# Filler matmuls, a transposed u in PSUM, earlier weights and another load order in the first batch of a recurrent-attention-plus-MLP kernel

## The chip, the cores and the metric

The kernel runs on one core of one Trainium2 chip. The metric is device time in microseconds (us). Medians are over all runs of a kernel, ratios over its fast runs alone. Most executions of one kernel agree within about 1%. A run that is over 1.5% above the fastest of the same kernel is marked slow and left out of the ratios. Engine names in the profile: PE is TensorE (matmul), PEld its weight load, DVE is VectorE, ACT ScalarE, POOL GpSimd, SP SyncE. An engine name with a q is its sequencer issuing a DMA. L325 is line 325 of that kernel's file, so the same operation has another line number in each kernel.

## The reference, cut to what matters

```
# q, k, v, alpha: [4, 8, 768, 48] float32
for t in range(S):                                   # gated linear recurrence, per batch and head
    state = alpha[:, :, t, :, None] * state + k[:, :, t] (outer) v[:, :, t]
    y[:, :, t] = q[:, :, t] @ state
x = y as [batch, 768, 384]
h = x^T @ U @ V                                      # low-rank token mix, rank 32
u = x + h^T
out = u + relu(u @ w_ch1) @ w_ch2                    # MLP 384 -> 1536 -> 384
```

The kernel handles the recurrence in chunks of 128 steps, six per batch and 24 in all. A chunk needs one tile each of alpha, k, q and v. A tile is 128 partitions of eight head rows of 192 bytes, 192 KB together.

## The kernel before

All operations are first put in a list with estimated durations. A small planner then simulates the engines at build time, and writes each engine's instructions in the order that it found. On the chip this order is fixed: an instruction whose data is late holds up everything behind it on its engine, even if that could run. For the planner, DMA is a pipe that serves in order: each input tile takes 1030 ns of it.

```python
    # the planner's DMA model, in Plan.run
            if eng == "SP":                          # input tiles and outputs, on the sync queue
                dma = max(dma, t + 600.0) + cost
                clock[eng] = max(t + 450.0, dma - 3500.0)
                end = dma + 1600.0
            elif op.mode == "DMA":                   # weights, issued by GpSimd
                clock[eng] = t + 1000.0
                dma = max(dma, t + 1000.0) + cost
                end = max(t + 1000.0 + cost, t) + 2000.0
    # ... cut ...
    io = Pool(slots("io", 36, [C, H, D], FP32))      # landing tiles of the inputs
    # ... cut ...
    nc.scalar.dma_start(u_in, moe_U.rearrange("(c p) r -> p c r", p=128))
    for g in range(4):                               # V four times, for four row groups
        nc.scalar.dma_start(v_in[32 * g : 32 * g + R, :], moe_V)
    # ... cut: one chunk, stage_gla(b, c) ...
        # lt = log(alpha), ScalarE; its cumulative sum over time by a triangular matmul on TensorE
        P.add({"ACT": 435}, lambda e: nc.scalar.activation(lt()[:, :, 0:D], at(), AF.Ln), ...)
            nc.tensor.matmul(cb()[:, 0:DM], lhsT=ut_ones, rhs=lt()[:, :, 0:D], ...)
        # ai = exp(-sum), aa = exp(sum); rk = k * ai, rq = q * aa; both transposed; scores; y
    # ... cut: the token mix, stage_mix(b) ...
        # H = V^T (U^T x); ub = x + H; ub transposed by TensorE into PSUM, copied to uT; then the MLP
    # ... cut: the weights, with the last chunk of batch 0 ...
                vt = tiles[b, c][3]                  # three parts of w_ch1 follow v(0,5)
                for i in range(3):
                    P.add({"POOL": 2000}, lambda e, i=i: f_w1(i), r=[vt], w=[("w1", i)], ..., mode="DMA")
                vt = tiles[1, 0][3]                  # three parts of w_ch2 follow v(1,0)
                for i in range(3):
                    P.add({"POOL": 2400}, lambda e, i=i: f_w2(i), r=[vt], w=[("w2", i)], ..., mode="DMA")
```

k(0,5) below means the k tile of batch 0, chunk 5.

## Time and profile before

| | before |
|---|---|
| median of 3 runs | 186.41 us (185.22 to 186.91) |
| profiled span | 186.9 us |
| first MLP matmul starts | 43.99 us |
| last y matmuls of batch 0 start | 36.56 us |

The page of the kernel before has these lines besides those that the prediction shows. The first is the input queue: packets, megabytes, and the time its packets took as a share of 16 DMA engines over the span. The second is the chain of work that ended last, by engine. The last two are issues: size of one, and median us from issue to landing.

```profile
q1 hardware_dynamic: 103296, 23.60, 60.5%
...
PE 72%; DVE 5%; DMA 3%; issue 1%; ACT 1%; DVEq 0%; ACTq 0%
...
io<-in_alpha_dram SPq DMA_DIRECT2D x24, 192.0 KB, 3.8
...
w_sb<-in_moe_w_ch_dram POOLq DMA_DIRECT2D x6, 384.0 KB, 10.2
```

The chain is TensorE work for 72% of the span, so the end was set by TensorE. The first line gives a figure that matters later: 60.5% of 16 times 186.9 us, over 103296 packets, is 17.5 ns per packet.

### The profile page before, as it was taken

Reading aid. Unit: us, or ns where it says so; the run is one execution under the profiler, and the core shown is the slowest. Engines: PE = TensorE matmul, PEld = TensorE weight load, DVE = VectorE, ACT = ScalarE, POOL = GpSimd, SP = SyncE. Lnnn points to the kernel's source line nnn. Section 1 sums busy time; section 2 is a strip of 40 time slices with the busy share of each in tenths; the row PEclk is TensorE's granted clock in tenths of the full one; section 3 lists DMA queues with packets and bytes.
Section 4 is the critical chain, followed back from the end, with each engine's and each line's share of the span. In section 5 each row is a group of like instructions: output and inputs, shape, how many; then the busy total and the mean of one; then the engine's idle time right before and its main releaser. Section 6 shows DMA issues by size and latency. Waiting matters only on the chain.

```text
span 186.9 us, 4147 instructions
## 1 busy us (share of the span) xinstructions
PE 163.1 (87%) x1592; PEld 105.7 (57%) x1592; DVE 93.5 (50%) x185; ACT 98.8 (53%) x229; POOL 57.4 (31%) x86
## 2 busy tenths in 40 slices
PE   0157878788999999889999969999999999999991
PEld 0135655455666666566666647667666466665660
DVE  1137665546810667489687395546665462100321
ACT  2423555436897445669788829215876200797000
POOL 4061445774130444444464309510700000000000
PEclk9999999999999999999999996999999999999999
DMA  6999999999996689899899989952000112200222
GB/s 135 212 201 216 200 192 196 182 198 186 187 192 137 137 208 214 186 219 204 163 195 183 193 174 221 209 173 84 4 0 0 46 42 84 84 4 0 84 84 86
DMA packets 107075, 26.71 MB, mean 143 GB/s; under 512 B 101168, under 2 KB 106928, under 8 KB 107056
## 3 DMA queue, kind: packets, MB, share of 16 engines
q1 hardware_dynamic: 103296, 23.60, 60.5%
q0 software_dynamic: 2784, 2.36, 8.0%
q10 hardware_dynamic: 976, 0.49, 1.2%
q8 instruction: 12, 0.20, 0.4%
q14 instruction: 7, 0.06, 0.1%
HBM read 24.08 MB, written 4.72 MB: 154 GB/s over the span
## 4 chain that ended last, share of the span: by engine, by line
PE 72%; DVE 5%; DMA 3%; issue 1%; ACT 1%; DVEq 0%; ACTq 0%
PE ps L472 25%; PE ps L496 25%; PE ps L337 5%; PE ps L358 3%; DMA io<-in_alpha_dram 3%; PE ps L409 3%; DVE pm L368 2%; PE ps L450 2%; DVE ub L441 2%; PE ps L308 2%; PE ps L440 2%; PE ps L383 1%; PE ps L407 1%; PE ps L381 1%; PE ps L311 1%
## 5 line engine op out<-in xcount | busy, mean ns | idle before, releaser
L472 PE MATMUL ps<-uT,w_sb 128*128 128x384 bf16 x288 | 51.9, 326 | 0.0
L496 PE MATMUL ps<-w_sb,h1t 128*128 128x384 bf16 x288 | 51.6, 326 | 0.0
L483 ACT ACTIVATE h1t<-ps 128x384 bf16<-128x384 f32 x78 | 37.8, 490 | 19.3 <-PE ps L472 19.2
L326 POOL TENSOR_TENSOR rk<-io,ai 128x384 bf16<-128x384 f32 x24 | 21.9, 912 | 49.7 <-ACT ai L319 44.4
L496 PEld LDWEIGHTS <-h1t 128*128 128x128 bf16 x288 | 26.6, 98 | 16.1 <-issue 0.3
L368 DVE TENSOR_TENSOR pm<-ps,maskc 128x512 bf16<-128x512 f32 x48 | 31.2, 685 | 8.1 <-PE ps L358 8.0
L472 PEld LDWEIGHTS <-w_sb 128*128 128x128 bf16 x288 | 26.3, 98 | 15.6
L503 DVE TENSOR_TENSOR ou<-ub,ps 128x384 f32<-128x384 bf16 x24 | 13.3, 554 | 34.4 <-PE ps L496 34.0
L301 ACT ACTIVATE lt<-io 128x384 bf16<-128x384 f32 x24 | 12.7, 529 | 12.7 <-DMA io<-in_alpha_dram 8.3
L319 ACT ACTIVATE ai<-ps 128x384 bf16<-128x384 f32 x24 | 11.9, 498 | 13.9 <-PE ps L311 6.8
L261 POOL CAST rv<-io 128x384 bf16<-128x384 f32 x24 | 13.1, 547 | 17.6 <-DMA io<-in_v_dram 17.6
L326 POOL TENSOR_TENSOR rq<-io,aa 128x384 bf16<-128x384 f32 x18 | 16.5, 915 | 2.1 <-PE ps L472 2.1
L308 PE MATMUL ps<-lt,ut_ones 128*128 128x384 bf16 x24 | 9.3, 391 | 8.6 <-ACT lt L301 8.5
L257 ACT CAST xb<-ps 128x384 bf16<-128x384 f32 x23 | 11.1, 482 | 9.7 <-PE ps L409 9.7
L393 DVE TENSOR_TENSOR st<-ps,tot 128x384 bf16<-128x384 f32 x20 | 11.1, 554 | 8.4 <-PE ps L383 8.4
L337 PE MATMUL ps<-ident,rk 128*128 128x128 bf16 x96 | 11.1, 249 | 2.8 <-POOL rk L326 2.8
L441 DVE TENSOR_TENSOR ub<-xb,ps 128x384 bf16<-128x384 bf16 x24 | 11.6, 547 | 2.6 <-PE ps L440 2.6
L409 PE MATMUL ps<-rv,pm 128*128 128x48 bf16 x192 | 10.6, 192 | 2.5 <-DVE pm L368 2.5
L358 PE MATMUL ps<-qt,kt 48*128 48x128 bf16 x192 | 10.8, 240 | 2.2 <-DVE qt L259 2.1
L485 DVE TENSOR_SCALAR h1t<-ps 128x384 bf16<-128x384 f32 x18 | 9.6, 556 | 6.1 <-PE ps L472 5.8
L257 ACT COPY kt<-ps 128x512 bf16<-128x512 bf16 x14 | 8.2, 588 | 7.8 <-PE ps L337 7.7
L337 PE MATMUL ps<-ident,rq 128*128 128x128 bf16 x96 | 10.8, 244 | 1.7 <-DVE rq L326 1.6
(52 smaller groups left out, 166.0 us busy)
## 6 DMA issues: line engine op xcount, KB each, us to landing
io<-in_alpha_dram SPq DMA_DIRECT2D x24, 192.0 KB, 3.8
io<-in_k_dram SPq DMA_DIRECT2D x24, 192.0 KB, 3.9
io<-in_q_dram SPq DMA_DIRECT2D x24, 192.0 KB, 3.9
io<-in_v_dram SPq DMA_DIRECT2D x24, 192.0 KB, 3.9
out_dram<-ou SPq DMA_DIRECT2D x24, 192.0 KB, 1.9
w_sb<-in_moe_w_ch_dram POOLq DMA_DIRECT2D x6, 384.0 KB, 10.2
v_in<-in_moe_V_dram ACTq DMA_DIRECT2D x4, 96.0 KB, 4.3
u_in<-in_moe_U_dram ACTq DMA_DIRECT2D x1, 96.0 KB, 3.6
```

What stands on the lines that cost most here:

```text
L257: nc.scalar.copy(dst, src)
L261: nc.gpsimd.tensor_copy(dst, src)
L326: eng.tensor_tensor(dst()[:, :, 0:D], a(), x(), op=ALU.mult)
L337: nc.tensor.matmul(t[:, p, :], lhsT=ring()[:, 2 * p : 2 * p + 2, :].rearrange("t h w -> t (h w)"), rhs=ident, start=True, stop=True, is_tr ...
L358: nc.tensor.matmul(sc[par]()[:, p * C : (p + 1) * C], lhsT=kT()[o : o + D, p, :], rhs=qT()[o : o + D, p, :], start=(p == 0), stop=(p == HP ...
L368: nc.vector.tensor_tensor(pm()[:, :, par, :], s2, maskc.to_broadcast([C, HP, C]), op=ALU.mult)
L409: nc.tensor.matmul(y[:, h * D : (h + 1) * D], lhsT=pm()[:, h // 2, h % 2, :], rhs=rv()[:, h, :], start=(h == 0 and sprev is None), stop=(h ...
L441: P.add({"DVE": 465}, lambda e, c=c, hb=hb: nc.vector.tensor_tensor(ub()[:, c, :], xb()[:, c, :], hb()[:, 0:DM], op=ALU.add), r=[hb, (xb, ...
L472: nc.tensor.matmul(hb()[:, 0:TW], lhsT=w1_sb[jt * 128 // FW][:, ct, jt * 128 % FW : jt * 128 % FW + 128], rhs=uT()[:, ct, tt * TW : (tt + ...
L483: nc.scalar.activation(dst, hb()[:, 0:TW], AF.Relu)
L496: nc.tensor.matmul(hb()[:, 0:DM], lhsT=h1()[:, jt, c * C : (c + 1) * C], rhs=w2_sb[jt // JW][:, jt % JW, :], start=(jt == 0), stop=(jt == ...
L503: P.add({"DVE": 468}, lambda e: nc.vector.tensor_tensor(ou(), ub()[:, c, :], hb()[:, 0:DM], op=ALU.add), r=[hb, (ub, c)], w=[ou], prio=-100)
```

## The change

Its intent: bring the MLP of batch 0 forward. TensorE runs cold and with gaps in the first batch, so fillers should keep its clock up. V is loaded once and spread to four row groups by a small matmul. The transposed u of batch 0 is built directly in PSUM. The weights are issued once k(0,5) has landed, earlier than before, and v of a chunk is loaded behind alpha, k and q of the next one, except in the last chunk of a batch. The planner's weight and tile costs are changed to match. The diff, cut:

```diff
@@ planner: weights have a pipe of their own beside the tiles'
             elif op.mode == "DMA":
-                clock[eng] = t + 1000.0
-                dma = max(dma, t + 1000.0) + cost
-                end = max(t + 1000.0 + cost, t) + 2000.0
+                clock[eng] = t + 900.0
+                big = max(big, t + 1500.0) + cost
+                dma = max(dma, t + 1500.0) + cost
+                end = big + 1600.0
@@ fillers in 60% of the planned TensorE gaps, up to 33 us of planned time
+        at = self.warm_from
         for op in order:
+            if op.eng == "PE" and op.t < self.warm_until:
+                n = int((op.t - at - 100.0) * self.warm_share / 216.0)
+                for _ in range(n):
+                    self.warm()
+            if op.eng == "PE":
+                at = op.t + op.engs["PE"]
             op.fn(op.eng)
@@ tiles
-    v_in = const.tile([128, S], FP32, name="v_in")
+    v_in = const.tile([R, S], FP32, name="v_in")
+    v_bf = const.tile([R, S], BF16, name="v_bf")
 ...
+    filler = const.tile([128, 512], BF16, name="filler")
+    nc.vector.memset(filler, 0.0)
+    tiny = const.tile([128, 1], FP32, name="tiny")
@@ loads
-            P.add({"SP": 1030.0}, lambda e: nc.sync.dma_start(t(), ...), w=[t], prio=key)
+            P.add({"SP": 965.0}, lambda e: nc.sync.dma_start(t(), ...), w=[t], prio=key)
 ...
-            for t, src, o in ((at, alpha, 0.0), (kt, k, 0.1), (qt, q, 0.2), (vt, v, 1.05)):
+            for t, src, o in ((at, alpha, 0.0), (kt, k, 0.1), (qt, q, 0.2), (vt, v, 1.25 if c < NC - 1 else 0.3)):
@@ scales and the cast of v on either of two engines in batch 0
-        P.add({"POOL": 885}, ... rk ...)
-        P.add({"DVE": 420} if b == 0 else {"POOL": 885}, ... rq ...)
+        both = {"DVE": 420, "POOL": 885} if b == 0 else {"POOL": 885}
+        P.add(both, ... rk ...)
+        P.add(both, ... rq ...)
@@ mix of batch 0: x transposed into PSUM, H^T accumulated on it, copied to uT (ub follows later)
+                def f_x(e, j, ...): nc.tensor.matmul(tb[j]()[...], lhsT=xb()[:, c, j * C : (j + 1) * C], rhs=ident, ...)
+                def f_h(e, j, ...): nc.tensor.matmul(tb[j]()[:, 0:TW], lhsT=utx()[:, j * C : (j + 1) * C], rhs=vm_sb[...], ...)
@@ weights
-                vt = tiles[b, c][3]
-                ... three parts of w_ch1 after v(0,5), three of w_ch2 after v(1,0)
+                kt = tiles[b, c][1]
+                P.add({"POOL": 100}, lambda e: nc.gpsimd.tensor_copy(tiny, kt()[:, 0, 0:1]), r=[kt], w=["gate"], prio=-1)
+                for i in range(2):
+                    P.add({"POOL": 2200 * (i + 1)}, lambda e, i=i: f_w1(i), r=["gate"], w=[("w1", i)], prio=-1, mode="DMA")
+                P.add({"POOL": 7000}, lambda e: f_w2(), r=["gate"], w=["w2"], prio=-1, mode="DMA")
```

## The prediction

> **What bounds the kernel now.** I read the busy tenths in 40 slices of the page first, to see whether one limit holds all along. It does not:
>
> ```profile
> PE   0157878788999999889999969999999999999991
> POOL 4061445774130444444464309510700000000000
> DMA  6999999999996689899899989952000112200222
> ```
>
> A slice is 4.67 us. From slice 9 (42 us) on the TensorE is full, and the DMA is full until 127 us. Before 42 us the TensorE shows 70 to 80% busy, which looks harmless; the by-line view of the two transposes of a chunk, taken for 12 to 40 us and again for 45 to 105 us, says what those tenths are made of (durations min/median/max in ns):
>
> ```profile
> L337 PE MATMUL ps<-ident,rk x22: 281/314/314, 11.8 to 33.0; 128*128 128x128 bf16 x22
> L308 PE MATMUL ps<-lt,ut_ones x6: 478/500/527, 12.0 to 35.1; 128*128 128x384 bf16 x6
> L337 PE MATMUL ps<-ident,rk x44: 218/219/230, 46.8 to 100.2; 128*128 128x128 bf16 x44
> L308 PE MATMUL ps<-lt,ut_ones x11: 322/326/326, 47.0 to 100.5; 128*128 128x384 bf16 x11
> ```
>
> The same instruction takes 314 ns early and 219 ns late, and 500 against 326: the array runs cold through the whole first batch. The difference for 384 columns, about 174 ns, is 384 columns at half rate against full rate. The timeline of the TensorE then shows the period of the recurrence and where warmth begins:
>
> ```profile
> 17.35 0.50 PE L308 MATMUL ps<-lt,ut_ones 128*128 128x384 bf16 x1
> 21.14 0.61 PE L358 MATMUL ps<-qt,kt 48*128 48x128 bf16 x8 [0.52 <-DVE qt L259]
> 21.68 0.50 PE L308 MATMUL ps<-lt,ut_ones 128*128 128x384 bf16 x1
> 26.01 0.50 PE L308 MATMUL ps<-lt,ut_ones 128*128 128x384 bf16 x1
> 38.64 2.08 PE L440 MATMUL ps<-utx,vm_sb 128*128 128x384 bf16 x6 [0.57 <-ACT utx L257]
> 43.99 1.14 PE L472 MATMUL ps<-uT,w_sb 128*128 128x384 bf16 x6
> ```
>
> A chunk takes 4.33 us (17.35 to 21.68 to 26.01). The bulk work, the first MLP matmul (L472), starts only at 43.99. The issues on the sync queue say whether data is late: alpha is issued every 3.95 us between 8.12 and 31.81, and the last input of batch 0 is issued at 25.16, some 3.9 us (the page's median landing) before it lands at about 29. Its y is finished only at 37.06 (copy xb). So the first batch is bound by a **chain of latencies in static order** (cumulative sum, exp, scale, transpose, copy out, scores, next sum), not by DMA alone. It also starts late; two waits show why (total us, times, longest):
>
> ```profile
> ACT lt L301 <- DMA io<-in_k_dram: 4.3, 1, 4.3
> POOL vm_sb L269 <- DMA v_in<-in_moe_V_dram: 5.0, 1, 5.0
> ```
>
> ScalarE spends 1.28 to 6.25 issuing four copies of V before its first log at 6.30, and GpSimd waits for the fourth copy (to 9.81) before it can scale the first k (10.60).
>
> After 44 us the end is set by TensorE throughput: the MLP matmuls are a half of the ending chain, 0.163 us each. Count it, with columns/2.4 GHz plus 2.5 ns each (the rate at which 72 matmuls took 11.70 us at the chain's end): a chunk 1.77 us, a mix 2.4 us, an MLP 144 x 0.1625 = 23.4 us per batch (72 + 72 matmuls). From 44 to 183 us lie four MLPs (93.6), some 17.5 chunks (31) and three mixes (7.2): 132 us of 139, so 7 us are lost. Two places hold most of it: 76 to 86 us, where MLP of batch 0 has run out and batch 1's mix is not ready, and 110.7 to 112.3, where the TensorE waits for an alpha tile.
>
> **What the Trainium skill says.** "TensorE: Matmul & The Clock Gate", Part 1: the array's default clock is half, released after some 3.4 us of sustained activity, lost after an idle window; back to back, a matmul takes N/1.2 ns cold and N/2.4 + 2.5 ns warm. The trace agrees: 174 ns difference for 384 columns against 157.5 by the formula, and six H matmuls at 38.64 span 2.08 us where later six take 1.14; the granted clock in the page reads 9 throughout and does not show this. "DMA: Bandwidth & Descriptors", Issuing engines are not separate DMA queues: all queues share the 16 engines and interleave. The trace agrees: once the weights are issued (32.5 to 38.7 us), the next input issues take 5.23, 5.42 and 4.14 us instead of about 0.9. "SBUF — State Buffer", Who interferes with whom: a VectorE instruction with two SBUF inputs contends with a GpSimd one that reads SBUF. The scale rq on VectorE takes 0.55 us alone and 0.73 to 0.81 beside a GpSimd scale here, so moving rk to VectorE too is not free of that.
>
> **The change part by part.**
>
> *Fillers.* Matmuls of 512 columns on zeros into a reserved eighth bank, 60% of the planned gaps up to 33 us of planned time. Planned free time is about 33 - 1.5 - 6 x 1.77 = 21 us; 60% of it by 0.216 is at most 58, fewer after rounding down, say 40. If they warm the array, each cycle loses 0.15 us in the sum, 0.1 to 0.2 in each of two transposes, 0.2 in the scores: about 0.6 of 4.33, so 3.7 us. Inputs at 3.85 us per chunk (four tiles of 0.965) then bind equally. The cost is delay where a real gap is shorter than planned, some tenths, mostly in the first 5 us while each cold filler takes 0.43 us.
>
> *V once, on the sync queue.* Removes 3 x 96 KB (1.5 tiles, some 1.4 us of DMA), frees ScalarE from 1.3 to 6.2 and GpSimd from its wait to 9.8. First log near 4.2 instead of 6.3; scores of chunk 0 near 8 to 9 instead of 12.7. Two selection matmuls and two copies rebuild V on four row groups (0.16 + 0.48 us each), off the path.
>
> *Load order and rk on either engine.* v(5) moves ahead of the next batch's alpha. Fitting the trace (28.5 tile equivalents landed by 28.6 us: 1.24 + 0.96 n), k(5) now lands near 22.4, q(5) 23.3, v(5) 25.2. Scale on VectorE 0.56 against 0.91.
>
> *First MLP.* Chain-limited, chunk 5's scores come 5 x 3.75 = 19 us after those of chunk 0, so at 27 to 28; data-limited at 25.5. Then masks 1.3, y 0.35, xb 0.5, utx 0.5, its copy 0.5, with hand-over about 0.1 each: H near 31.
>
> *u transposed in PSUM.* Before: H 38.64, ub adds, transposes, copies, MLP at 43.99, 5.35 us. After: x transposed by identity ahead of time (18 matmuls), H accumulated on it (six times 0.16), three copies of 0.5 us per half on two engines: about 1.5 us. The six ub matmuls and adds (1.0 us of TensorE) stay but move behind.
>
> So the first MLP matmul moves from 44.0 to **32.5** (30.5 to 35): 11.5 us gained.
>
> *Weights.* Issued after k(5), near 22.5 to 24. All take about 14 us of DMA (the tiles slow from 32.5 to 52 while some five come through). First part (512 columns) lands near 29, second near 34, needed 2 us after the start, third by 42, needed 12 us after. Just in time. Input tiles for batch 1 now starve from 24 to 42 rather than 33 to 52.
>
> **The sum.** Of 11.5 us, 1.0 goes back for ub and 0.8 for the sums and transposes of batch 1 that used to precede 44 us. That leaves 9.7. Batch 1 ends landing at 41.5 + 20.5 x 0.98 = 61.6, plus 9 us of chain, so its mix ends at 70 to 72, where before it ended at 85.5; the TensorE needs 32.5 + 23.4 + 1 + 10.6 = 67.5 plus bubbles. So 2 to 4 us of waiting remain at that hand-over, slightly fewer than before. From there to the end 97 to 99 + 3.9 us tail: 173 to 176; alternatively 186.4 - 9.7 = 176.7. I choose **175.5 us** (-5.9%).
>
> **The rivals.** *DMA becomes the bound.* Alpha of batch 3's fourth chunk landed at 111.7; with 1.5 us less V and no sync-queue stall (56.8 to 61.6, where an output in queue order blocks input issues) it lands near 106, 5 us earlier, while the TensorE arrives 10 us earlier. Static order then puts the difference into waits: 0 to 4 us, giving up to 180. For it: tiles took 1.05 us each from 85 to 106 us while the new plan assumes 0.965. Against it: TensorE still has batch 2's MLP to run, if it is ordered first. *Fillers don't warm, or delay.* The array was up to 80% busy and still cold. Then the period stays near 4.2, MLP starts at 36 and runs cold for its first microseconds: 179 to 180. *Weights late.* If batch 1's tiles keep the weights from coming, MLP stalls at its second part by 2 to 4 us: 178 to 180. *More gain.* If the hand-over to batch 1 loses nothing and alpha is in time, the 7 us lost shrink to 4: 171.
>
> **Range and chances.** Most rivals cost less than the 9.7 us; all together would be needed to lose them. Range 170.5 to 181. Two per cent is 182.7: faster 0.91, same 0.07, slower 0.02.
>
> **What would show it.** Transposes of 219 ns before 30 us (warm); first log at 4 to 5; L472's first matmul at 32.5 with copies of uT straight after H; the weight tile waited for not at all; mix of batch 1 done near 71; a TensorE wait for alpha near 106. I am wrong if the early transposes stay at 314, if the MLP starts after 36, or if waits for input tiles past 60 us add to more than 8 us.

## The result

| | before | after |
|---|---|---|
| median | 186.34 us (4 runs) | 198.67 us (4 runs, 197.25 to 199.83) |
| profiled span | 186.9 us | 197.4 us |
| last y matmuls of batch 0 start | 36.56 us | 33.01 us |
| first MLP matmul starts | 43.99 us | 51.43 us |
| from there to the end of the span | 142.9 us | 146.0 us |

The changed kernel is **slower**, by a ratio of 1.067 (95% interval 1.056 to 1.077). Here and below, a ratio is the mean time of one kernel's fast runs over that of the other's in the same rounds, so not quite the ratio of the medians quoted. The predicted time was 175.5 us, with a range up to 181.

Of the 10.5 us between the two profiled spans, 7.4 lie before the first MLP matmul and 3.1 after it. Yet batch 0's recurrence ended 3.5 us earlier. So something came in between.

### The profile after

The page of the changed kernel, lines that answer to those of before (tenths in 40 slices of 4.93 us; PEclk is the granted clock in tenths):

```profile
PE   6976978006999999989988997599999999999991
...
PEclk9999589655999999999999999969999999999999
DMA  6999999999993199999999989942200012200222
...
q1 hardware_dynamic: 104128, 23.80, 65.7%
...
PE 35%; SPq 23%; issue 17%; DMA 11%; POOL 10%; ACT 1%; DVE 1%; POOLq 0%; ACTq 0%
...
io<-in_alpha_dram SPq DMA_DIRECT2D x24, 192.0 KB, 4.5
...
w_sb<-in_moe_w_ch_dram POOLq DMA_DIRECT2D x1, 1152.0 KB, 17.5
```

The two zeros in the PE line are a hole of some 11 us, from 35 to 46 us, while DMA is full. PEclk falls to 5 or 6 in the hole and right behind it, and once before, around 20 to 25 us. It is no sure sign of a cold array: in the kernel before it reads 9 all through the first batch, where transposes take 314 ns. The DMA line has a hole of its own at slices 12 and 13 (59 to 69 us). The chain that ended last is no longer mostly TensorE: the sync queue's issues (SPq) take 23%. And the input queue's packets take 65.7% of 16 times 197.4 us over 104128, which is 19.9 ns each, where before had 17.5.

The timeline of TensorE around the hole (start, length, the group, in brackets the idle time before it and what ended that):

```profile
33.01 0.35 PE L434 MATMUL ps<-rv,pm 128*128 128x48 bf16 x7 [0.40 <-DVE pm L393]
...
34.44 0.39 PE L362 MATMUL ps<-ident,rk 128*128 128x128 bf16 x4
46.14 0.48 PE L332 MATMUL ps<-lt,ut_ones 128*128 128x384 bf16 x1 [11.31 <-ACT lt L325]
...
46.59 1.44 PE L473 MATMUL ps<-vm_sb,utx 128*128 128x384 bf16 x4
...
51.43 1.79 PE L521 MATMUL ps<-uT,w_sb 128*128 128x384 bf16 x10
```

L473 is H accumulated on the transposed x of **batch 0**, and everything it needs is there at about 35 (the copy utx ends at 34.92). In front of it stands L332, the cumulative sum of chunk (1,1), of the **next batch**. It waits 11.31 us for a log, and the timeline of ScalarE says why the log is late:

```profile
45.56 0.52 ACT L325 ACTIVATE lt<-io 128x384 bf16<-128x384 f32 x1 [12.47 <-DMA io<-in_alpha_dram]
```

GpSimd's timeline shows what filled the DMA in this time, and the sync queue's shows the alpha tile's issue:

```profile
27.40 0.19 POOL L564 COPY tiny<-io 128x1 f32<-128x1 f32 x1 [2.56 <-DMA io<-in_q_dram]
27.53 1.71 POOL L299 DMA_DIRECT2D w_sb<-in_moe_w_ch_dram  x2
29.24 1.05 POOL L302 DMA_DIRECT2D w_sb<-in_moe_w_ch_dram  x1
```

```profile
28.89 1.00 SPq L310 DMA_DIRECT2D io<-in_alpha_dram  x1
29.93 2.68 SPq L310 DMA_DIRECT2D io<-in_k_dram  x1
32.66 9.14 SPq L310 DMA_DIRECT2D io<-in_q_dram  x1
...
57.91 0.75 SPq L310 DMA_DIRECT2D io<-in_v_dram  x1
67.18 0.37 SPq L552 DMA_DIRECT2D out_dram<-ou  x1
```

Alpha(1,1) was issued at 28.89, between the weights, and used at 45.56: some 16.7 us from issue to landing, where the median is 4.5. The later lines show the follow-up. Between 58.7 and 67.2 the sync queue issues nothing. Next in its order stands the first output of batch 0, which is late because the MLP is; 8.5 us, where the same stall before took 4.7. This is the hole in the DMA line.

The sums of waits (total us, times, longest), first of the kernel before, then of the changed one:

```profile
ACT lt L301 <- DMA io<-in_alpha_dram: 8.3, 6, 3.6
```

```profile
ACT lt L325 <- DMA io<-in_alpha_dram: 23.9, 12, 12.5
...
PE ps L332 <- ACT lt L325: 12.9, 4, 11.3
```

What the change was made for did work. The by-line view of the transposes of rk, and of the fillers, from 5 us (durations min/median/max in ns):

```profile
L362 PE MATMUL ps<-ident,rk x24: 219/253/314, 6.0 to 29.6; 128*128 128x128 bf16 x24
```

```profile
L273 PE MATMUL ps<-filler x29: 376/390/634, 1.2 to 33.2; 128*128 128x512 bf16 x29
```

The fillers warm the array, though not all along: 219 ns is the warm transpose, 314 the cold one, and those that start between 19.66 and 25.8 us are slow again.

### The profile page after: what moved, and what is told of

It is laid out like the page before. It is cut to its first block, busy times and chain, and to the rows that moved or that the text cites. A ratio compares the mean times of both kernels' runs of the same rounds, so it can differ in the third digit from the quotient of the medians.

```text
span 197.4 us, 4236 instructions
## 1 busy us (share of the span) xinstructions
PE 168.4 (85%) x1629; PEld 104.3 (53%) x1629; DVE 94.9 (48%) x188; ACT 102.7 (52%) x237; POOL 53.5 (27%) x83
## 3 DMA queue, kind: packets, MB, share of 16 engines
q1 hardware_dynamic: 104128, 23.80, 65.7%
## 4 chain that ended last, share of the span: by engine, by line
PE 35%; SPq 23%; issue 17%; DMA 11%; POOL 10%; ACT 1%; DVE 1%; POOLq 0%; ACTq 0%
SPq L310 22%; PE ps L544 18%; PE ps L521 12%; DMA io<-in_alpha_dram 9%; POOL rq L350 4%; POOL rk L350 4%; POOL rv L284 2%; DMA io<-in_k_dram 2%; PE ps L482 1%; PE ps L362 1%; PE ps L383 1%; PE ps L492 1%; SPq L287 1%; ACT lt L325 0%; PE ps L332 0%
## 5 line engine op out<-in xcount | busy, mean ns | idle before, releaser
L531 ACT ACTIVATE h1t<-ps 128x384 bf16<-128x384 f32 x84 | 40.4, 492 | 24.9 <-PE ps L521 24.8
L521 PE MATMUL ps<-uT,w_sb 128*128 128x384 bf16 x288 | 50.8, 326 | 0.4 <-ACT uT L280 0.4
L350 POOL TENSOR_TENSOR rk<-io,ai 128x384 bf16<-128x384 f32 x22 | 20.1, 913 | 59.4 <-ACT ai L343 59.4
L350 POOL TENSOR_TENSOR rq<-io,aa 128x384 bf16<-128x384 f32 x21 | 19.2, 914 | 10.4 <-DMA io<-in_q_dram 6.7
L332 PE MATMUL ps<-lt,ut_ones 128*128 128x384 bf16 x24 | 8.4, 353 | 13.0 <-ACT lt L325 12.9
L284 POOL CAST rv<-io 128x384 bf16<-128x384 f32 x18 | 9.1, 506 | 17.3 <-DMA io<-in_v_dram 14.9
L282 DVE COPY qt<-ps 128x512 bf16<-128x512 bf16 x16 | 6.8, 423 | 13.2 <-PE ps L362 13.2
L273 PE MATMUL ps<-filler 128*128 128x512 bf16 x29 | 11.0, 495 | 1.2 <-DVE offd L241 1.2
L362 PE MATMUL ps<-ident,rq 128*128 128x128 bf16 x96 | 10.2, 234 | 2.0 <-DVE rq L350 1.5
L344 ACT ACTIVATE aa<-ps 128x384 bf16<-128x384 f32 x24 | 11.9, 495 | 0.0
L362 PE MATMUL ps<-ident,rk 128*128 128x128 bf16 x96 | 10.0, 231 | 1.3 <-DVE rk L350 0.8
L434 PE MATMUL ps<-rv,pm 128*128 128x48 bf16 x192 | 9.2, 185 | 1.7 <-DVE pm L393 0.9
## 6 DMA issues: line engine op xcount, KB each, us to landing
w_sb<-in_moe_w_ch_dram POOLq DMA_DIRECT2D x1, 1152.0 KB, 17.5
```

The costliest lines, as they stand in the source:

```text
L284: nc.gpsimd.tensor_copy(dst, src)
L344: P.add({"ACT": 390}, lambda e: nc.scalar.activation(aa().rearrange("t h d -> t (h d)"), cb()[:, 0:DM], AF.Exp), r=[cb], w=[aa], prio=pr + ...
L350: eng.tensor_tensor(dst()[:, :, 0:D], a(), x(), op=ALU.mult)
L362: nc.tensor.matmul(t[:, p, :], lhsT=ring()[:, 2 * p : 2 * p + 2, :].rearrange("t h w -> t (h w)"), rhs=ident, start=True, stop=True, is_tr ...
L521: nc.tensor.matmul(hb()[:, 0:TW], lhsT=w1_sb[i][:, ct, o : o + 128], rhs=uT()[:, ct, tt * TW : (tt + 1) * TW], start=(ct == 0), stop=(ct = ...
L531: nc.scalar.activation(dst, hb()[:, 0:TW], AF.Relu)
```

## The experiments

Three suspects came out of the traces.

- **A, order:** two or three instructions of batch 1 stand in front of the mix of batch 0, and their tiles are overtaken by the weights. Rival: the weights, issued early, are simply too much for the DMA, whatever the order.
- **D, pace:** with the MLP started early, input tiles become the bound, and the planner's 965 ns per tile puts tile-dependent work too early. Rival: the start of the MLP carries over one to one.
- **E, alignment:** packets became slower by 2.4 ns on average. The only difference to the landing tiles is their place in memory: `tiny`, one float per partition, is padded to 32 bytes and shifts the 36 landing tiles from byte 41536 (a multiple of 64) to 44384 (32 beside one), together with the other new tiles. (The builds of the two kernels give these addresses.) Rival: more queues at work, another mix of reads and writes.

Below, E-free means `tiny` made 16 floats wide, so that the tiles start at a multiple of 64 again. The kernels ran beside the kernel before; its medians there were between 186.7 and 187.1 us.

**e1_order.** Two instructions are held behind MLP matmuls of batch 0 in the order: the log of (1,1) and the scale rq of (1,0), which the trace also showed waiting.

```diff
-  lt: ..., prio=pr + 40, slack=sl)
+  lt: ..., prio=pr + 40, slack=sl, after=[m1[1, 6]] if (b, c) == (1, 1) else ())
-  rq: ..., prio=pr + 11, slack=sl)
+  rq: ..., prio=pr + 11, slack=sl, after=[m1[0, 10]] if (b, c) == (1, 0) else ())
+  # m1[tt, jt] is the MLP matmul group of batch 0
```

> Only the order of issue differs from the changed kernel: the log of alpha of batch 1's second chunk is planned after the 19th MLP block of batch 0, and the scale of q of its first chunk after the 11th, so that no instruction that needs a tile caught behind the weights stands in front of the mix and the MLP of batch 0. Theory A (the loss is an in-order wait of TensorE and ScalarE, 11.3 us at 34.8 to 46.1 us of the changed kernel's trace, and the 8.5 us stall of the sync queue that follows from it): the first MLP matmul moves from 51.4 to 36 to 38 us, the sync queue's stall at 58.7 to 67.2 shrinks to under 2 us, the time falls from 198.7 to 178 to 186 us. Theory B (early weights starve batch 1 of input and the time is lost there in any order): the MLP starts early but the wait turns up later, the time stays over 193 us. Theory C (fillers or the new way to build u cost it): over 195 us.

Measured: 189.95 us, where I expected 178 to 186; ratio to before 1.015 (1.008 to 1.022). The timeline of TensorE in this run:

```profile
33.90 0.82 PE L474 MATMUL ps<-vm_sb,utx 128*128 128x384 bf16 x4
34.56 1.14 PE L483 MATMUL ps<-utx,vm_sb 128*128 128x384 bf16 x6
...
36.20 2.11 PE L522 MATMUL ps<-uT,w_sb 128*128 128x384 bf16 x12
39.40 0.82 PE L522 MATMUL ps<-uT,w_sb 128*128 128x384 bf16 x4 [1.08 <-DMA w_sb<-in_moe_w_ch_dram]
```

The MLP starts at 36.20 instead of 51.43, and the hole in the DMA line is gone. So A is shown: two ordering edges, with the same weights at the same place, take the hole away. But 15 us of earlier start gave some 9 us of time. The kernel is still slower than before, although its MLP starts 7.8 us earlier. The waits say where it went:

```profile
ACT lt L326 <- DMA io<-in_alpha_dram: 24.1, 18, 2.6
```

No long wait is left, but 18 short ones. From 80 to 130 us TensorE is idle for 6.3 us (50 less 43.7 busy), where before had 2.4 in one profile and 1.0 in another.

**e2_w2_late.** The changed kernel, with the 1152 KB of second weights issued only after alpha(1,1) has landed.

```diff
-  P.add({"POOL": 7000}, lambda e: f_w2(), r=["gate"], ...)
+  P.add({"POOL": 100}, ... tensor_copy(tiny, alpha(1,1)) ..., w=["gate2"])
+  P.add({"POOL": 7000}, lambda e: f_w2(), r=["gate2"], ...)
```

> Only the second weight matrix is held back, until alpha of batch 1's second chunk has landed; the instruction order is otherwise left to the planner, with that alpha's sum still in front of the last part of the mix. Theory A with weights as the cause of the late alpha: alpha lands near 36 to 38 instead of 45.6 us, the first MLP matmul comes at 38 to 41 instead of 51.4, the second weight matrix lands near 50 and is just in time; 186 to 191 us. If the alpha's delay is not due to the weights ahead of it: alpha still lands after 44 us and the time stays within 2 us of 198.7.

Measured: 190.2 us, 1.019 (1.015 to 1.023). The line of the waiting sum:

```profile
40.96 0.48 PE L332 MATMUL ps<-lt,ut_ones 128*128 128x384 bf16 x1 [5.99 <-ACT lt L325]
```

The wait halves, to 5.99 us, with 1152 KB fewer in front. The alpha landed at about 40.4, later than the 36 to 38 that I expected, and the MLP began at 45.87, not at 38 to 41: the first weights, issued at 27.80 ahead of this alpha (29.30), are left to hold it up.

**e3_nofill.** The changed kernel without fillers (`warm_share = 0.0`).

> The changed kernel without any filler matmul; order otherwise the same. Theory A: fillers have nothing to do with the loss, the 11 us wait for alpha stays; the recurrence of batch 0 runs cold and its last y comes 0 to 3 us later, which the wait hides; 197 to 201 us. Theory C (fillers delay the recurrence or slow the input transfers, whose last k of batch 0 landed at 27.3 us where 22.4 was predicted): that k lands 2 us or more earlier and the time falls under 195 us.

Measured: 195.98 us, 1.042 (1.032 to 1.052), with two fast runs (193.32 and 195.67). That misses the 197 to 201 of theory A. The profile was taken in a slow run, so I use only that the long wait is still there (8.68 us) and that the gate copy runs at 27.52, no earlier than the 27.40 of the changed kernel: what theory C said of k(0,5) isn't seen. Fillers are not the main thing that makes the change slow. But the interval lies clear of the changed kernel's (1.056 to 1.077), so in that kernel the fillers may cost some 2%; on another chip and with two fast runs, and why is left open.

**e4_before_w_early.** The other way round: the kernel before, with only the weights moved, gated by `tiny` on k(0,5).

```diff
-  r=[vt] (v(0,5) for w_ch1, v(1,0) for w_ch2)
+  r=["gate"], with tensor_copy(tiny, k(0,5)) writing "gate", and tiny = const.tile([128, 1], FP32)
```

> The kernel before with one part of the change alone: all six weight transfers are issued when the last k of batch 0 has landed, not after the last v and the next batch's first v. Its planner puts the sum of batch 1's second chunk in front of the mix of batch 0 as well. Theory A: that sum waits for its alpha behind the weights, TensorE idles 5 to 12 us before the mix, the first MLP matmul moves from 44 to 48 to 52 us, time 190 to 196 us. Rival (early weights help, something else in the change hurts): MLP at or before 44 us, time 183 to 187 us.

Measured: 187.63 us, 1.006 (1.000 to 1.011). This is a miss: I expected 190 to 196. The wait is there but short:

```profile
37.26 0.48 PE L309 MATMUL ps<-lt,ut_ones 128*128 128x384 bf16 x1 [1.49 <-ACT lt L302]
```

But the edit did not do what it was made for. GpSimd's timeline, first of before, then of this run with the sync queue's alpha(1,1), shows the first weights issued at 32.28 where before has 32.49. The gate's copy stands in GpSimd's fixed order behind a scale of rk, which runs at 31.30. (The last three weights came 2.4 us earlier, at 34.76.)

```profile
32.49 2.47 POOL L275 DMA_DIRECT2D w_sb<-in_moe_w_ch_dram  x3
```

```profile
30.61 0.99 SPq L287 DMA_DIRECT2D io<-in_alpha_dram  x1
...
32.28 2.48 POOL L276 DMA_DIRECT2D w_sb<-in_moe_w_ch_dram  x3
```

So alpha(1,1) was issued ahead of the weights here, where the changed kernel has it behind them, and it was not overtaken. This run says nothing of an early issue; e14 comes at that question from the other side. This run also has `tiny`, and its packets took 20.4 ns (71.1% of 16 times 185.5 us over 103296), which put me on E.

**e5_order_pace.** e1 with the planner told that tiles take 1100 ns from batch 1 on.

```diff
-  P.add({"SP": 965.0}, ...)
+  P.add({"SP": 965.0 if b == 0 else 1100.0}, ...)      # plus the edges of e1
```

> The order run (MLP of batch 0 ahead of the tiles caught behind the weights) with one more edit: from batch 1 on, the planner counts 1100 ns for an input tile, not 965, which is what tiles took in the order run (alpha to alpha 4.6 us per chunk of four tiles from 54 to 114 us, seven outputs among them). Theory D (once the MLP starts early, the static order built on a pace of 965 ns makes TensorE wait for tiles that are not there; the order run idles 6.3 us between 80 and 130 us, the kernel before 2.4): idle there falls to under 3.5 us, the time from 190 to 184 to 187 us. If instead TensorE runs out of work because input transfers bound it in any order: idle only moves to 65 to 85 us, before the mix of batch 1, and the time stays at 188.5 to 192.

Measured: 184.73 us, 0.987 (0.981 to 0.994). The MLP starts at 36.21, as in e1, and idle time from 80 to 130 us falls from 6.3 to 1.1. The wait that was 24.1 us in e1:

```profile
ACT lt L326 <- DMA io<-in_alpha_dram: 5.7, 7, 1.8
```

Nothing on the chip was made faster; tile-dependent work only stands later in the order, behind MLP work that could run. D is supported, for a kernel with the offset of E in it; e12 below asks what is left without.

**e7_before_pace.** The kernel before with the optimistic 965 ns from batch 2 on.

```diff
-  P.add({"SP": 1030.0}, ...)
+  P.add({"SP": 1030.0 if b < 2 else 965.0}, ...)
```

> The kernel before, with only the planner's figure for an input tile of batches 2 and 3 lowered from 1030 to the 965 ns of the changed kernel; its first 60 us are the same instructions in the same order. Theory D: chunks of batches 2 and 3 are ordered earlier than their tiles land, waits for tiles after 80 us grow by 1 to 4 us, time 187.5 to 191. If the pace is harmless: within 1 us of the kernel before.

Measured: 184.79 us, 0.989 (0.983 to 0.996), where I expected slower. So 965 is not harmful by itself here. In before, TensorE reaches the MLP about 8 us later than its own plan (44.0 against a planned 35.6), so tiles that are late by the plan are there anyway. D holds only where the MLP starts early. Why this one gained 1% is left open.

**e8_before_fill.** The kernel before with the fillers alone.

> The kernel before with the filler matmuls and their reserved bank alone. If they warm the array: transposes of batch 0 at about 219 ns instead of 314 for most of the time from 9 to 38 us, the mix 1 to 3 us earlier, the first MLP matmul at 41 to 43 us. What the time does tells what an earlier start alone is worth: theory D says under half of it, 185 to 187 us; if TensorE throughput alone set the end, all of it, 183.5 to 185.

Measured: 185.13 us, 0.990 (0.979 to 1.001). The cumulative sums of neighbouring chunks start 3.73 us apart (17.68, 21.41, 25.14), where before has 4.33, and the MLP starts at 40.31, 3.7 us earlier. That is the prediction's own figure for fillers. But the 3.7 us gave about 1.8 us of time (by the interval, 0 to 3.9).

**before_again.** A second profile of the kernel before, for packet times and landings.

> The kernel before, unchanged, profiled on the same chip as the other three, to see how much of the input rate (3.85 us per chunk between 8 and 20 us in the first profile, 4.3 in the run of the kernel before with early weights) belongs to the chip and not to the edit. Expected: 4.1 to 4.4 us per chunk, and the first MLP matmul again at 43.5 to 45.5 us.

Measured: 186.04 us (one run, state unknown), MLP at 43.78, 17.7 ns per packet. So 17.5 was no accident of one profile. Alphas were issued every 3.86 us (7.88 to 19.45), not 4.1 to 4.4 as I expected: the slower input of e4 belongs to that kernel and not to the chip.

**e9_after_align.** The changed kernel, E-free.

```diff
-    tiny = const.tile([128, 1], FP32, name="tiny")
+    tiny = const.tile([128, 16], FP32, name="tiny")     # and the copy goes to tiny[:, 0:1]
```

> The changed kernel with one number different: the scratch tile that gates the weights is 16 floats wide, not 1. Tiles are padded to 32 bytes, so the one-float tile moves all later tiles, the 36 input tiles among them, from a start that is a multiple of 64 bytes to one 32 bytes beside it; 16 floats move them by 64. Theory E: that offset makes each input packet dearer. Packet time on the input queue, worked out from its share of the span, is 17.5 to 17.8 ns in the four profiles of kernels without the one-float tile and 19.9 to 20.7 in the six with it. Expected by E: 17.4 to 18 ns a packet, the last k of batch 0 lands near 25 instead of 27.3 us, the first MLP matmul comes 2 to 3 us earlier (48 to 50; the in-order wait for alpha remains), the waits for tiles after 80 us shrink, 189 to 195 us. If E is wrong: 19.9 to 20.7 ns and 197 to 200 us.

Measured: 193.45 us, 1.032 (1.023 to 1.041). The input queue's line of this run (span 191.0 us):

```profile
q1 hardware_dynamic: 104128, 23.80, 58.5%
```

That is 17.2 ns per packet against 19.9 of the changed kernel, by nothing but 60 unused bytes per partition. These are means. Counted from the packet records in the two trace files, the median packet of an input row takes 15 ns in both kernels; what differs is how many take over 20 ns, 22.5% in the changed kernel and 3.1% in e9. My expectation for the start of the MLP failed, though: 51.57, not 48 to 50. The order still holds it, with waits of 3.38 and 9.79 us; the gain came later.

**e10_before_shift.** The kernel before with an unused tile of 32 bytes ahead of the landing tiles.

```diff
+    const.tile([C, 8], FP32, name="shift")
     io = Pool(slots("io", 36, [C, H, D], FP32))
```

> The kernel before with an unused tile of 32 bytes in front of the input tiles and nothing else: same instructions, same order. Theory E: 20 to 20.7 ns a packet, chunks of batch 0 arrive every 4.2 to 4.4 us instead of 3.8. As its TensorE is late against its own plan, most of this is hidden: 187 to 190 us against 186.5. If E is wrong: 17.5 to 17.8 ns a packet and no difference.

Measured: 193.03 us, 1.023 (1.013 to 1.033). The input queue's line (span 195.6 us, slow):

```profile
q1 hardware_dynamic: 103296, 23.60, 67.6%
```

20.5 ns per packet; e4, in a fast run, had 20.4. One unused tile costs this kernel 2.3% (two fast runs, 190.75 and 191.79), more than the 187 to 190 us that I expected. e4, with the same offset, was only 0.6% slower than before, so the cost in time is less sure than that per packet. E is shown from both sides: in every profile with the offset, packets take 19.9 to 20.7 ns (after, e1 to e5, e10), in every one without it 17.1 to 17.8 (twelve profiles).

**e11_order_pace_align** is e5, E-free. **e12_order_align** is e1, E-free, so with 965.

> Order, pace of 1100 ns and the aligned scratch tile together. Theory E with theory A: first MLP matmul at 33.5 to 35.5 us, last input issued near 113 instead of 119.8, but the pace is now too slow for the tiles, so the planner holds chunks back; 180 to 183.5 us.

> Order and the aligned scratch tile, the pace left at the changed kernel's 965 ns. If the waits after 80 us of the order run (6.3 us between 80 and 130) came from tiles slowed by the offset, they fall to under 3 us here although the pace is 965: first MLP matmul at 33.5 to 35.5 us, 179 to 183 us, at least 6 us under the order run's 190. If the pace itself is at fault: waits stay over 4.5 us and the time is 184 to 188.

Measured: e11 181.87 us, 0.966 (0.958 to 0.975); e12 185.75 us, 0.975 (0.963 to 0.986), with runs from 181.0 to 188.5. Both profiles fell into slow runs. e11's MLP started at 39.98, where I expected 33.5 to 35.5, because of a third overtaken instruction:

```profile
35.09 0.61 PE L363 MATMUL ps<-ident,rk 128*128 128x128 bf16 x4 [3.65 <-POOL rk L351]
```

This is rk of (1,0), whose k tile the weights overtook. e12 is too noisy to part pace from alignment: its slow profile idles 3.5 us from 80 to 130, between my two marks (under 3, over 4.5). But its fast runs, 181.0 and 183.4, show most of e1's loss gone at a pace of 965. So D is shown only for tiles that the offset slows; what the pace is worth without it stays open.

**e13_order2_pace_align.** e11 with this third edge, and a pace of 1050.

```diff
-  rk: ..., prio=pr + 10, slack=sl)
+  rk: ..., prio=pr + 10, slack=sl, after=[m1[0, 8]] if (b, c) == (1, 0) else ())
```

> The best version the runs point to: order, aligned scratch tile, a pace of 1050 ns after batch 0, and one more scale (k of batch 1's first chunk) planned after the 9th MLP block, because in the aligned runs the weights overtake that tile too and TensorE waits 3.7 us for it at 31 to 35 us. First MLP matmul at 35 to 37 us instead of 40; 179.5 to 182.5 us, 2.5 to 4 per cent under the kernel before. If input transfers bound it now, the 4 us are lost again before the mix of batch 1 and the time stays at 181.5 to 183.

Measured: 180.45 us (six runs, 180.1 to 181.0), 0.966 (0.961 to 0.971), the change's parts all in it. Its page, and its TensorE timeline at the start of the MLP:

```profile
PE   5977777899999996899999899999999999999990
...
DMA  5999999999999899998989999931000122100222
...
q1 hardware_dynamic: 104128, 23.80, 62.6%
```

```profile
35.81 6.50 PE L522 MATMUL ps<-uT,w_sb 128*128 128x384 bf16 x39
```

The zeros are gone from PE, and the hole from DMA. The MLP runs from 35.81 without a wait, packets take 17.2 ns, and idle time from 80 to 130 us is 0.9. Against e11 the MLP starts 4.2 us earlier, but the ratio is the same: the third edge and the pace of 1050 bought no time that these runs can tell.

**e14_w_late_align.** The changed kernel, E-free, old order, but all weights gated on alpha(1,1). If early weights are the fault, this should cure it.

```diff
-                kt = tiles[b, c][1]
+                kt = tiles[1, 1][0]
```

> The changed kernel, aligned, with all weights held until alpha of batch 1's second chunk has landed, some 5 to 7 us later than now; no order edit. If the early issue of the weights as such is the fault: no wait over 2 us, MLP at 37 to 39 us, 183 to 187 us. If the fault is that the planner believes tiles issued around the weights come in queue order: its order now puts the sum of the third chunk of batch 1 in front of the mix, that alpha is the one overtaken, TensorE waits 6 to 12 us for it, MLP at 46 to 50 us, 189 to 195 us.

Measured: 194.02 us, 1.041 (1.032 to 1.050). The MLP began at 38.73, then:

```profile
51.28 0.48 PE L408 MATMUL ps<-rv,rk 128*128 128x96 bf16 x4 [11.29 <-POOL rv L284]
```

Another instruction, a v tile in place of the alpha tile (I had expected alpha again), the same wait of 11.3 us: v(1,1) was issued at 33.60, beside the weights (32.15 to 34.90), and cast at 50.73. Later weights only move the victim. The weights go out as late here as in the kernel before (32.49), which has no such wait; so it isn't the early issue as such that costs, but an order with batch 1's work ahead of the MLP. The fault is that the plan expects a tile issued beside the weights in its turn, and the DMA doesn't deliver it so.

**e15_e13_nofill.** e13 without fillers.

> The best version without fillers: what the fillers are worth once nothing else covers them. Transposes of batch 0 at 314 ns again, first MLP matmul 2 to 4 us later (the same fillers moved it 3.7 us in the kernel before), and 0.5 to 2.5 us more in time, since half or more of an earlier start is given back to input transfers.

Measured: 182.07 us, 0.975 (0.970 to 0.981), MLP at 38.43, transposes of 314 ns. The fillers bring the MLP 2.6 us forward, worth 1.6 us of time.

**e16_best_rows256** and **e17_best_28.** A rival within E: perhaps what counts is how many 256-byte blocks a 192-byte row touches. e16 is e13 with 28 landing tiles whose rows start 256 bytes apart on a 256-byte boundary; e17 is e13 with 28 tiles packed as before, its control.

> The best version with 28 input tiles, their rows of 192 bytes laid 256 bytes apart from a start that is a multiple of 256 (the control has rows back to back from a multiple of 64). Same instructions in the same order. If a write costs by the 256-byte blocks it touches (Trainium skill, DMA: Bandwidth & Descriptors, How a descriptor splits into AXI transactions, which says it of reads): by its beats, 9 a row on average in the control and 6 here, so packet time falls from 17.2 towards 12 to 14 ns, inputs finish many us earlier and the time falls by 2 us or more. If only a start that is not a multiple of 64 is dear: 17 to 17.5 ns and the control's time within 1 us.

> The control: the best version with 28 input tiles, rows back to back. 17.2 ns a packet and 180.5 us within 1 us, as the planner gives the same order for 28 tiles as for 36.

Measured: e16 179.86 us, 0.962 (0.955 to 0.968), 17.1 ns per packet; e17 180.25 us, 0.963 (0.956 to 0.970), 17.2 ns. No difference: rows within one block gain nothing. What costs is a start 32 bytes beside a multiple of 64; no other offset was tried.

The steps in one table (ratio to before):

| order edges | pace | offset of 32 bytes | run | ratio |
|---|---|---|---|---|
| no | 965 | yes | the change | 1.067 |
| no | 965 | no | e9 | 1.032 |
| two | 965 | yes | e1 | 1.015 |
| two | 1100 | yes | e5 | 0.987 |
| two | 965 | no | e12 (noisy) | 0.975 |
| two | 1100 | no | e11 | 0.966 |
| three | 1050 | no | e13 | 0.966 |

## Why the prediction was wrong

Point by point, by the prediction's own steps.

**Fillers: right.** Warm transposes of 219 ns before 30 us, and in e8 a period 0.6 us shorter, as predicted. There were 29 fillers, not 40. In the changed kernel itself the period was not 3.75, however: its sums start at 11.85, 17.17, 22.66 and 27.59, 4.9 to 5.5 us apart. Over the same chunks the E-free e9 has 4.2 to 4.7, so a part of this is the offset. As for the rest, ScalarE's static order has a cast of v ahead of the next log, and v now comes last; casts waited 4.1 us for v tiles in all. I tested no kernel for this, so it stays argued.

**V once, and u built transposed: right.** The first log came at 3.71 (predicted "near 4.2"). H to first MLP matmul takes 2.3 us in e1 (33.90 to 36.20), where before took 5.35; predicted was 1.5.

**"Fitting the trace … k(5) now lands near 22.4": wrong.** It landed at about 27.3 (the gate copy runs at 27.40), and in the E-free e9 at about 25.0. So some 2.4 us of this are the offset, and some 2.6 a fit that promised too much. The offset stood in the diff, as a tile of one float, and I did not ask where the tiles behind it would land. It goes on through the whole run: 2.4 ns a packet, over 104128 packets and 16 engines, is 15.6 us of DMA time, in a kernel whose DMA was full until 127 us.

**"Just in time. Input tiles for batch 1 now starve from 24 to 42": the step that failed.** I had seen that tiles would starve, and took that for a delay of batch 1 alone. But instructions that need those tiles stand ahead of batch 0's mix in TensorE's order, so their delay is batch 0's. The prediction's sum gives back 0.8 us for sums and transposes of batch 1 "that used to precede 44 us", as if they all moved behind the MLP; in the trace L332 and L362 of batch 1 still stand in front of it, at 31.64, 34.44, 46.14 and 47.82. The prediction put the first MLP matmul at 32.5; it came at 51.43. Of the 18.9 us, 11.3 are this wait, 3.7 are in e1 as well (a later end of the recurrence, 2.3 us instead of 1.5), and 3.9 are a cold array after the hole (six H matmuls take 2.02 us, in e1 1.14) with batch 1 work between. The late MLP then made the output late, and the sync queue stood for 8.5 us, where the prediction had counted "no sync-queue stall".

The trace shows how a tile loses its turn. Counted from its packet records, between 35 and 45 us the DMA engines moved 1677 packets of input rows and 1669 of weights, one for one, but 0.32 MB of the first and 1.54 MB of the second: an input row is 192 bytes, a weights packet 768 to 2048. That agrees with the Trainium skill, "DMA: Bandwidth & Descriptors", Queues, rings and completion order: each DMA engine takes turns between queues, a packet at a time. The alpha tile, 1024 such rows behind others, took 16.7 us to land. Neither before nor after does the plan know this: it assumes that a tile issued between the weights comes in its turn. The weights themselves landed 7 to 17.5 us after their issue, and in e1 the MLP waited 1.08 us for one part: this part of the step was nearly right.

**"That leaves 9.7": wrong in size.** The sum let an earlier MLP come off the end nearly one to one. The changed kernel can't show this term, as its MLP came later; the other runs say less, and not by a fixed share. In e8 3.7 us earlier gave 1.8, within noise of none and of all; in e15 2.6 gave 1.6. In e1 7.8 us earlier gave nothing, since idle time in the middle took it; e12 puts most of that down to the offset. The named rival "DMA becomes the bound" fits e1; no named rival had the wait ahead of the mix. With order, pace and alignment mended, the gain is 3.4% in place of 5.9%. In e13, TensorE is idle for 0.9 us between 80 and 130 and starts its MLP 8.2 us sooner than before, for a median 6.6 us below: about four fifths come through. One sum doesn't come out either, though nothing hangs on it: 70 to 72 plus 97 to 99 plus 3.9 is 171 to 175, not 173 to 176. And the granted clock of the page before doesn't read 9 throughout: one slice, 126 to 131 us, reads 6.

**What would have shown it wrong, it did, in part.** Of the prediction's own alarms, "MLP starts after 36" went off by 15 us. The one for waits "past 60 us" did not: TensorE's waits on tiles and their casts and scales there add to about 5 us, and the wait that cost most came at 35 to 46. The early transposes did not stay at 314.

## What to carry to other kernels

In a statically ordered program, a bulk transfer delays not only what needs it but whatever shares the DMA with it; put instructions that depend on tiles issued beside it behind work that has its data already. After adding a small tile, check where the tiles behind it start: here one float per partition slowed the input queue's packets by 16 to 19% on average (19.9 against 17.2 ns between the change and e9, 20.7 against 17.3 between e5 and e11). An earlier start is worth only what the next bound leaves, so ask which tiles it will now meet before they have landed.

## What the Trainium skill lacked or had wrong

- **Start of a landing tile.** "SBUF — State Buffer", Operand start alignment, states which starts are legal and says itself that it timed nothing. The runs show a cost: 192-byte rows landing at 32 bytes beside a multiple of 64 took 19.9 to 20.7 ns per packet on average, at a multiple of 64 they took 17.1 to 17.8. An unused 32-byte tile made the kernel before 2.3% slower (e10), and 60 unused bytes took the changed one from 1.067 to 1.032 (e9). The nearest in the skill is the section that e16's expectation names, on 256-byte blocks in reads; e16 laid the rows on such blocks and its packets took 17.1 ns against 17.2. No page that I read has the cost at 32 bytes.
- **How much a small-row stream loses.** The place on queues and turns cited above explains the direction and gives no size. Here the turns were one for one in packets, 0.32 against 1.54 MB in 10 us, and a tile of 192-byte rows took up to 16.7 us to land, where the median is 4.5.
- **Transposes and the clock.** "TensorE: Matmul & The Clock Gate", Part 4, gives about 275 ns for a 128x128 transpose within a kernel and says that the full clock does not engage for it. Here it takes 219 ns when the array is warm and 314 when it is cold. Whether transposes alone would warm the array no run shows.
